# Batch 0's q and k loaded as float32 from SyncE's queue and cast on chip, in a dilated sliding-window attention with a SiLU feed-forward layer

## The chip, the cores and the metric

The kernel runs on one core of a Trainium2 chip. The metric is the device time of the kernel in microseconds (us), the median of three runs. Before the change it is 321.23 us (320.72 to 321.88). The profiled execution of the kernel before has a span of 319.5 us, and TensorE was granted its full clock in it. Line numbers (L127) are those of the kernel before.

## What is computed

Attention over 8 batches, 8 heads, 576 positions and 64 features, followed by a feed-forward layer over the 4608 tokens (model width 512, inner width 2048). All inputs and the output are float32.

```python
rel = pos[:, None] - pos[None, :]
mask_plain = (rel >= 0) & (rel < 32)                       # heads 0 to 3
mask_dil = (rel >= 0) & (rel < 128) & (rel % 4 == 0)       # heads 4 to 7
scores = where(mask, q @ k.T / sqrt(64), -1e9)
attn_out = softmax(scores) @ v
x = attn_out.transpose(0, 2, 1, 3).reshape(4608, 512)
h = x @ w_in
out = (h / (1 + exp(-h))) @ w_out
```

## The kernel before, in words

**Work and data.** Everything on chip is float16, and matmuls accumulate in float32. Attention goes batch by batch. The plain heads work in blocks of 96 queries against 128 keys. The dilated heads are split into the four residues of the position modulo 4, so that a dilated window of 128 becomes a plain window of 32 among 144 positions (`M`). The feed-forward layer goes over groups of 512 tokens, of which the first is split in two of 256 (`GROUPS`). For each group, layer 1 makes 16 blocks of `h` (L861, four matmuls each), ScalarE takes the tanh (L870), VectorE makes `gT` (L872), and layer 2 (L894) needs all 16 blocks of `gT` and `w_out`.

**Batch 0.** Its q and k are loaded by GpSimd's DMA queue with a cast from float32 to float16 on the way (`issue_part`, L125). `issue_first` (L131, called at L191 and L192) loads rows 0 to 95 (`MA`) of the 144 for the dilated heads and then for the plain heads, k before q; `k0` (L226) loads the last 48 rows of both into one tile, the "rest". TensorE transposes these tiles against the identity: `TD` (L529, `trans_d0`) for the dilated heads, `TA` (L554, `trans_a0`) for the plain ones, `TR` (L540) and `TS` (L567) for the rest. Batch 0's masks come as a bias that a matmul with the identity adds to the scores (L595). The scores are exponentiated by ScalarE (L616, L620), multiplied with V (L656) and divided (L659, L660), and the result is transposed into `xA` (L698, L710), the input of layer 1.

**Loads and their order.** GpSimd issues all loads of the first part of the run, in the order of the program: q and k of batch 0, the identity and the band of the masks (made by GpSimd itself), a first half of V for the dilated heads (`vraw`, L200), V for the plain heads (`vp`, L201), and then the list `ORDER` (L55, walked from L216): `k0` the rest of q and k, `r0` the second half of `vraw`, `w0a` to `w3` the four parts of `w_in`, `c0` a cast-free copy of the second half of `vraw` into the tile `vd` on GpSimd (L232), `d1` and `p1` q and k of batch 1 (dilated and plain heads), `r1` and `v1` its V, and `o0` to `o3` the parts of `w_out`. The instruction at L232 waits for the transfer of `r0`, and everything that stands behind it in GpSimd's program waits with it. Batch 2 is loaded by `third_batch` at the end of batch 0. Batches 3 to 7 take another path: their q and k are cast into DRAM (L137) and read back transposed by SyncE (L151, L154).

**The plan.** While the program is built, a planner fixes the order of the instructions: it keeps an estimated time, takes the next step that its estimates say is ready, and chooses ScalarE or VectorE for copies by which of them would be done first (`best`, L483). When loads land is part of these estimates: `LOAD_US` and `AT_W0` (L56, L57) give the landing times of the list, and `AT_DIL`, `AT_PLAIN`, `AT_VRAW`, `AT_VP`, `AT_REST`, `AT_V1` (L332 to L338) those of the first loads. On the chip every engine runs its instructions in the planned order and waits where an estimate was too early. Batch 0's own order of steps is the list at L721: `TD`, `S` (scores), `TA`, `V` (the copy into `vd`), `D` and `P` (the products with V of the dilated and plain heads), `XD` and `XP` (the transposes into `xA`), `TR`, `TS`.

Of the kernel before, what the change touches and what calls it, by code (L numbers as in the profile page):

```python
# [16 lines left out]
def kernel(  # L17
# [9 lines left out]
    nc = tc.nc  # L27
# [26 lines left out]
    BIG = 32768.0  # L54
    ORDER = "k0 r0 w0a w0b c0 w1 w2 w3 d1 p1 r1 o0 v1 o1 o2 o3".split()  # L55
    LOAD_US = {"w": 2.75, "o": 2.6, "d": 3.7, "p": 3.7, "r": 1.4, "v": 2.6, "k0": 2.0, "r0": 1.2, "c0": 0.0, "w0a": 1.4, "w0b": 1.4}  # L56
    AT_W0 = 10.6  # L57
    BIASED = (0,)
# [35 lines left out]
    kPs = [cpool.tile([P, HP // 2, W + S], F16, name=f"kP_{i}") for i in range(2)]  # L94
    pairs = {
        key: cpool.tile([MA, HP // 2, DIL, 2, D], F16, name=f"pair_{key}")
        for key in ("k", "q", "rest")
    }
    fence = cpool.tile([P, 4], F16, name="fence")
# [6 lines left out]
    def nat_of(b, key):  # L106
        i = ("k", "q", "rest").index(key)
        return nats[b % 2][:MA, i * RW : (i + 1) * RW].rearrange("p (h r d) -> p h r d", h=H, r=DIL)
# [15 lines left out]

    def issue_part(src, m0, m1, dst, h0, h1):  # L125
        rows = src[0].rearrange("h (m r) d -> m h (r d)", r=DIL)
        nc.gpsimd.dma_start(  # L127
            out=dst[: m1 - m0, h0:h1].rearrange("p h r d -> p h (r d)"), in_=rows[m0:m1, h0:h1]
        )

    def issue_first(h0, h1):  # L131
        issue_part(k, 0, MA, nat_of(0, "k"), h0, h1)
        issue_part(q, 0, MA, nat_of(0, "q"), h0, h1)

# [45 lines left out]

    for t in vraws[::-1]:
        nc.vector.memset(t, 0.0)
    nc.vector.memset(vps[0][:W, 0, :], 0.0)
    nc.vector.memset(kqDs[0][:, :, :, 0, MA:], 0.0)
    for t in vps:
        nc.vector.memset(t[:, :, D:], 1.0)
    for t in vds:
        nc.vector.memset(t[:, :, :, :, D:], 1.0)
    for t in kPs:
        nc.vector.memset(t[:, :, :W], 0.0)  # L190
    issue_first(HN, H)  # L191
    issue_first(0, HN)  # L192
    make_identity(nc, ident)
    nc.gpsimd.memset(band, 1.0)
    for s, base in ((1, 0), (-1, W - 1)):
        nc.gpsimd.affine_select(
            out=band, in_=band, compare_op=ALU.is_ge, fill=0.0, base=base,
            pattern=[[s, P]], channel_multiplier=-s,
        )
    issue_vraw(0, (0,))  # L200
    issue_vp_first()  # L201
    nc.vector.tensor_scalar(band, band, 1.0, BIG, ALU.subtract, ALU.mult)
    nc.vector.tensor_copy(mask_d[:, :6], band[:, None, :MH].broadcast_to([P, 6, MH]))
    nc.vector.tensor_copy(mask_d[:, 6:], band[:, None, P - MH :].broadcast_to([P, 4, MH]))
    nc.vector.tensor_copy(mask_p, band[:, None, W:].broadcast_to([P, 6, QB]))
    nc.vector.memset(mask_p[:W, :2], -BIG)
    for t in probs:
        c = 2 * 4 * MH
        n = PW + P - c
        nc.scalar.copy(t[:, c:], vraws[1].rearrange("p a h r d -> p (a h r d)")[:, :n])  # L210

    wi = moe_w_in.rearrange("(c p) f -> p c f", p=P)
# [3 lines left out]
    for what in ORDER:  # L216
        kind, n = what[0], int(what[1])
        if kind == "w":
            f0, f1 = {"": (0, 4), "a": (0, 2), "b": (2, 4)}[what[2:]]
            cols = slice((4 * n + f0) * P, (4 * n + f1) * P)  # L220
            nc.gpsimd.dma_start(out=w_in16[:, :, cols], in_=wi[:, :, cols])  # L221
        elif kind == "o":
            nc.gpsimd.dma_start(
                out=w_out16[:, 4 * n : 4 * n + 4], in_=wo[:, 4 * n : 4 * n + 4]
            )
        elif what == "k0":  # L226
            issue_part(k, MA, M, nat_of(0, "rest"), 0, H)
            issue_part(q, MA, M, nat_of(0, "rest")[MR:], 0, H)
        elif what == "r0":
            issue_vraw(0, (1,))  # L230
        elif what == "c0":
            nc.gpsimd.tensor_copy(vds[0][:, 1, :, :, :D], vraws[0][:, 1])  # L232
        elif kind == "d":
            issue_nat(n, HN, H)
        elif kind == "p":
            issue_nat(n, 0, HN)
        elif kind == "r":
            issue_vraw(n)
        else:
            issue_vp(n)  # L240
        at += LOAD_US[what] if what in LOAD_US else LOAD_US[kind]
        AT[what] = at
        if kind == "w":
            for f in range(f0, f1):
                AT_WIN[4 * n + f] = at
# [18 lines left out]
    class Plan:  # L264
        def __init__(self):
            self.t = 0.0
            self.now = 0.0
            self.free = {"ACT": 0.0, "DVE": 0.0}
            self.heap = []
            self.n = 0  # L270
            self.rings = {nm: [] for nm in RINGS}
# [59 lines left out]
    t2 = at  # L331
    AT_DIL = {0: 5.4, 1: AT["d1"], 2: t2 + 7.0}  # L332
    AT_PLAIN = {0: 7.5, 1: AT["p1"], 2: t2 + 7.0}
    AT_VRAW = {0: 8.6, 1: AT["r1"], 2: t2 + 8.6}
    AT_VP = {0: 10.6, 1: AT["v1"], 2: t2 + 11.4}
    AT_CAST = t2 + 18.0
    AT_REST = AT["k0"]
    AT_V1 = AT["r0"] + 1.2  # L338
    AT_WOUT = [AT[f"o{n}"] for n in range(4)]
# [96 lines left out]
    def attention(b):  # L436
# [91 lines left out]

        def trans_d0(ring, h):  # L529
            tps = small(ring, [P, 4, MA], F16, f"td_{b}_{h}")  # L530
            for n in range(4):
                nc.tensor.transpose(
                    tps[:, n],
                    nat_of(b, "kq"[n % 2])[:, HN + h, n // 2 * 2 : n // 2 * 2 + 2, :], ident[:MA, :MA],
                )
            step = best(0.34, 0.42)
            yield step
            copy_on(step[0], kqD[:, h].rearrange("p r k m -> p (r k) m")[:, :, :MA], tps)

# [101 lines left out]
        def vd_of(ab):  # L641
            if b == 0 and ab == 1:
                return
            step = best(0.335, 0.95) if pe_path else ("DVE", 0.335)
            yield step
            copy_on(step[0], vd[:, ab, :, :, :D], vraws[b % NV][:, ab])
# [73 lines left out]
        if b == 0:  # L720
            order = [  # L721
                ("TD", 0), ("TD", 1), ("TD", 2), ("TD", 3), ("S", 3), ("S", 4), ("TA", 0, "k"),
                ("TA", 1, "k"), ("TA", 0, "q"), ("TA", 1, "q"), ("V", 0), ("D", 0, 0), ("D", 0, 1),
# [30 lines left out]
        for key in order:  # L754
# [9 lines left out]
            elif kind == "TA" and b == 0:  # L764
                st = Step(
                    lambda ring, a=a: trans_a0(ring, *a), 0.36, rings,
                    [AT_PLAIN[0]],
                )
            elif kind == "TD" and b == 0:
                st = Step(lambda ring, a=a: trans_d0(ring, *a), 0.17, rings, [AT_DIL[b]])  # L770
            elif kind == "TR":
                st = Step(lambda ring: trans_d1(ring), 0.34, rings, [AT_REST])
            elif kind == "TS":
                st = Step(lambda ring, a=a: trans_a1(ring, *a), 0.36, rings, [AT_REST])
            elif kind == "TA":
# [227 lines left out]
```

## Time and profile before

| engine or queue | busy in the span of 319.5 us |
|---|---|
| TensorE (PE), matmuls | 299.9 us (94%) |
| VectorE (DVE) | 195.1 us (61%) |
| ScalarE (ACT) | 163.6 us (51%) |
| GpSimd (POOL) | 54.5 us (17%), 87 instructions |
| DMA | 44.49 MB moved, 139 GB/s on average |

| stretch, us | TensorE busy | VectorE busy | ScalarE busy | GpSimd busy |
|---|---|---|---|---|
| 0 to 5 | 0.00 | 2.42 | 4.18 | 3.67 |
| 5 to 10 | 2.12 | 1.17 | 2.34 | 4.93 |
| 10 to 15 | 5.00 | 1.83 | 3.07 | 1.71 |
| 15 to 20 | 4.13 | 2.82 | 3.96 | 1.75 |
| 20 to 25 | 3.96 | 4.02 | 3.58 | 4.84 |
| 25 to 30 | 4.26 | 3.73 | 3.63 | 1.02 |
| 30 to 35 | 3.00 | 2.75 | 1.89 | 3.41 |
| 35 to 40 | 4.19 | 4.88 | 4.22 | 5.00 |

The page and the trace show one execution. "Busy" is the time in which an engine had an instruction under way; DMA issues on GpSimd are shown as instructions of about 0.7 us each. Matmuls overlap, so a busy TensorE need not be at its peak. A casting load is counted by the bytes that it writes, which are half of those that it reads. The chain of waits is followed back from the last instruction to what released each step; the waits view lists for each line what ended its idle time. The first transposes of batch 0 (L532) start at 5.26 us, the first scores (L595) at 9.98, the first matmul of layer 1 (L861) at 20.30 and the first of layer 2 (L894) at 41.12.

### The profile page before, as it was taken

How to read it: one execution, taken by the hardware profiler on the slowest of the kernel's cores; microseconds unless marked ns; L12 is line 12 of the kernel's file. 1: busy time of each engine (PE TensorE's matmuls, PEld its weight loads, DVE VectorE, ACT ScalarE, POOL GpSimd, SP SyncE). 2: the span in 40 equal slices, each digit the busy share in tenths (PEclk: the TensorE clock that was granted, in tenths of full speed). 3: DMA queues.
4: the chain of work that ended last, by engine and by line, in shares of the span. 5: the costliest groups of instructions: out<-in, count | busy, mean ns of one | idle time of the engine just before them, and what ended most of it. 6: DMA issues, size and time to landing. Idle time of an engine off the chain costs nothing.

```text
span 319.5 us, 6092 instructions
## 1 busy us (share of the span) xinstructions
PE 299.9 (94%) x2378; PEld 152.7 (48%) x2378; DVE 195.1 (61%) x493; ACT 163.6 (51%) x300; POOL 54.5 (17%) x87
## 2 busy tenths in 40 slices
PE   2797689999999999999999999999999999999994
PEld 1466575655445444544454444444444444444442
DVE  4367798899679777843895787548841553355000
ACT  7586665566665365453563564546452453355111
POOL 8473923000900031004100500000000000000000
PEclk9999999999999999999999999999999999999999
DMA  7999999999999959997999799952191000100221
GB/s 90 157 130 202 197 191 199 209 202 169 100 203 208 224 108 190 208 201 143 184 236 209 130 193 173 212 129 73 51 182 42 28 35 33 66 33 2 81 83 66
DMA packets 107124, 44.49 MB, mean 139 GB/s; under 512 B 73304, under 2 KB 102488, under 8 KB 107096
## 3 DMA queue, kind: packets, MB, share of 16 engines
q0 software_dynamic: 48960, 19.92, 51.6%
q1 hardware_dynamic: 52952, 14.75, 26.3%
q10 hardware_dynamic: 5184, 9.44, 8.4%
q8 instruction: 18, 0.29, 0.4%
q14 instruction: 10, 0.08, 0.1%
HBM read 39.84 MB, written 18.28 MB: 182 GB/s over the span
## 4 chain that ended last, share of the span: by engine, by line
PE 84%; DMA 8%; POOL 4%; ACT 2%; DVE 1%; issue 1%; ACTq 0%; POOLq 0%
PE y L894 38%; PE h L861 36%; PE s L607 3%; DMA w_in<-in_moe_w_in_dram 3%; DMA vraw<-in_v_dram 3%; DMA w_out<-in_moe_w_out_dram 2%; PE av_p L656 2%; PE av_d L656 2%; POOL nat L127 1%; ACT ob L905 1%; POOL vraw L161 1%; POOL vp L179 0%; POOL w_in L221 0%; DVE gT L872 0%; PE td L518 0%
## 5 line engine op out<-in xcount | busy, mean ns | idle before, releaser
L894 PE MATMUL y<-w_out,gT 128*128 128x512 f16 x576 | 138.6, 379 | 1.7 <-ACT ob L905 1.1
L872 DVE SCALAR_TENSOR_TENSOR gT<-th,h 128x512 f16<-128x512 f32 (+1 forms) x160 | 98.6, 628 | 59.3 <-ACT th L870 59.1
L870 ACT ACTIVATE th<-h 128x512 f32<-128x512 f32 (+1 forms) x160 | 88.4, 555 | 82.0 <-PE h L861 78.0
L861 PEld LDWEIGHTS <-w_in 128*128 128x128 f16 x640 | 58.0, 97 | 56.9 <-DMA w_in<-in_moe_w_in_dram 3.0
L894 PEld LDWEIGHTS <-gT 128*128 128x128 f16 x576 | 53.8, 98 | 61.2 <-issue 2.0
L861 PE MATMUL h<-xR,w_in 128*128 128x512 f16 x320 | 78.0, 379 | 0.2 <-DVE gT L872 0.2
L861 PE MATMUL h<-xA,w_in 128*128 128x512 f16 (+1 forms) x320 | 65.4, 337 | 3.0 <-DMA w_in<-in_moe_w_in_dram 2.1
L616 ACT ACTIVATE probs<-s 128x768 f16<-128x768 f32 (+2 forms) x47 | 36.5, 776 | 19.4 <-PE s L607 16.8
L905 ACT ACTIVATE ob<-y 128x512 f32<-128x512 f32 x36 | 21.5, 598 | 39.9 <-PE y L894 39.8
L660 DVE TENSOR_TENSOR oD<-av_d,rcps 72x256 f16<-72x256 f32 x64 | 26.9, 420 | 2.2
L656 PEld LDWEIGHTS <-probs 128*128 128x128 f16 x448 | 22.1, 99 | 11.9 <-issue 0.4
L660 DVE TENSOR_TENSOR oP<-av_p,rcps 96x256 f16<-96x256 f32 x48 | 20.2, 420 | 1.6
L397 POOL COPY fence<-kqT 128x1 f16<-128x1 f16 x10 | 2.0, 206 | 97.5 <-DMA kqT<-kq_s 97.5
L659 DVE RECIPROCAL rcps<-av_p 96x4 f32<-96x4 f32 x48 | 8.3, 174 | 13.1 <-PE av_p L656 12.7
L625 DVE TENSOR_TENSOR probs<-probs,mask_p 128x768 f16<-128x768 f16 x21 | 11.6, 552 | 6.0 <-ACT probs L616 5.9
L656 PE MATMUL av_d<-vd,probs 128*128 128x65 f16 x256 | 14.2, 196 | 0.3 <-ACT qP L479 0.3
L659 DVE RECIPROCAL rcps<-av_d 72x4 f32<-72x4 f32 x64 | 10.9, 171 | 5.0 <-PE av_d L656 5.0
L656 PE MATMUL av_p<-vp,probs 128*128 128x65 f16 x192 | 13.1, 194 | 0.2 <-ACT probs L620 0.2
L625 DVE TENSOR_TENSOR probs<-probs,mask_d 128x576 f16<-128x576 f16 (+1 forms) x23 | 11.8, 513 | 2.0 <-ACT probs L616 1.8
L161 POOL DMA_DIRECT2D vraw<-in_v_dram x16 | 11.0, 688 | 6.6 <-DVE rcps L659 2.3
L174 POOL DMA_DIRECT2D vp<-in_v_dram x7 | 10.0, 1431 | 2.1 <-PE av_p L656 1.8
L481 DVE COPY vd<-vraw 128x1024 f16<-128x1024 f16 x14 | 6.2, 440 | 4.5 <-DMA vraw<-in_v_dram 4.5
(86 smaller groups left out, 139.5 us busy)
## 6 DMA issues: line engine op xcount, KB each, us to landing
out_dram<-ob ACTq DMA_DIRECT2D x36, 256.0 KB, 3.7
kq_s<-in_k_dram POOLq DMA_DIRECT2D x5, 576.0 KB, 11.5
kq_s<-in_q_dram POOLq DMA_DIRECT2D x5, 576.0 KB, 15.1
vp<-in_v_dram POOLq DMA_DIRECT2D x7, 384.0 KB, 8.7
w_out<-in_moe_w_out_dram POOLq DMA_DIRECT2D x4, 512.0 KB, 11.4
vraw<-in_v_dram POOLq DMA_DIRECT2D x8, 224.0 KB, 5.6
w_in<-in_moe_w_in_dram POOLq DMA_DIRECT2D x3, 512.0 KB, 8.1
x_s<-oP SPq DMA_DIRECT2D x10, 144.0 KB, 3.8
```

Source lines behind the costliest of these rows:

```text
L161: nc.gpsimd.dma_start(out=vraw[p0 : p0 + m1 - m0, ab].rearrange("p h r d -> p h (r d)"), in_=src[m0:m1],)
L174: nc.gpsimd.dma_start(out=vps[b % NV][:, :, :D], in_=v_win(b * H * S - W, HN * NB, QB * D))
L616: nc.scalar.activation(p2, both[:, :, :n], AF.Exp, scale=scale)
L625: nc.vector.tensor_tensor(p2, p2, mk, ALU.mult)
L656: nc.tensor.matmul(a[:, i, : D + 1], lhs(i), rhs(i), start=True, stop=True)
L659: nc.vector.reciprocal(rcp[:n], a[:n, :, D : D + 1])
L660: nc.vector.tensor_tensor(o, a[:n, :, :D], rcp[:n, :, None].broadcast_to([n, HN, D]), ALU.mult)
L861: nc.tensor.matmul(h[:, :w], w_in16[:, c, f * P : (f + 1) * P], x_g[:, c], start=(c == 0), stop=(c == HP - 1),)
L870: nc.scalar.activation(th[:, :w], h[:, :w], AF.Tanh, scale=0.5)
L872: nc.vector.scalar_tensor_tensor(gTs[g][:, f, :w], th[:, :w], 1.0, h[:, :w], ALU.add, ALU.mult)
L894: nc.tensor.matmul(y, gTs[g][:, f, tb * P : (tb + 1) * P], w_out16[:, f], start=(f == 0), stop=(f == NFF - 1),)
L905: nc.scalar.activation(ob, y, AF.Copy, scale=0.5)
```

## The change

Batch 0's q and k are no longer loaded by GpSimd with a cast. SyncE's queue, which has no other work at that time, loads them as float32 with eight DMAs into six pieces of scratch (`stages`). The scratch is laid over tiles that are not used so early: the three `xR` tiles, the two `kqT` tiles and the tiles `pair`, which become one tile for that. On-chip casts then make the float16 tiles: four of them (rows 0 to 95: k and q of the dilated heads, k and q of the plain heads) are steps `C` of the plan, on VectorE or ScalarE; the two of the rest are `c4` and `c5`, on GpSimd, in the list behind `w3`. `k0` and `c0` leave the list; the second half of `vraw` is copied into `vd` by a step of the plan, as the first half is. The making of the mask tiles on VectorE is cut in two parts (steps `K`) that stand between the casts, and `TD` transposes k and q in separate steps, so that k can go ahead of q. The estimates of the plan are set anew. The purpose is to have GpSimd's queue issue only V and the weights, and to start its issues earlier.

```diff
...
-    ORDER = "k0 r0 w0a w0b c0 w1 w2 w3 d1 p1 r1 o0 v1 o1 o2 o3".split()
-    LOAD_US = {"w": 2.75, "o": 2.6, "d": 3.7, "p": 3.7, "r": 1.4, "v": 2.6, "k0": 2.0, "r0": 1.2, "c0": 0.0, "w0a": 1.4, "w0b": 1.4}
-    AT_W0 = 10.6
+    ORDER = "r0 w0a w0b w1 w2 w3 c4 c5 d1 p1 r1 o0 v1 o1 o2 o3".split()
+    LOAD_US = {"w": 2.6, "o": 2.6, "d": 3.1, "p": 3.1, "r": 1.4, "v": 2.5, "r0": 1.2, "w0a": 1.3, "w0b": 1.3, "c4": 0.0, "c5": 0.0}
+    AT_W0 = 9.8
+    AT_STAGE = (3.7, 4.9, 6.2, 7.6, 13.0, 14.5)
...
-    pairs = {
-        key: cpool.tile([MA, HP // 2, DIL, 2, D], F16, name=f"pair_{key}")
-        for key in ("k", "q", "rest")
-    }
+    pair_all = cpool.tile([MA, 3, HP // 2, DIL, 2, D], F16, name="pair_all")
+    pairs = {key: pair_all[:, i] for i, key in enumerate(("k", "q", "rest"))}
+    homes = [
+        xRs[0].rearrange("p a b -> p (a b)"),
+        xRs[1].rearrange("p a b -> p (a b)"),
+        xRs[2].rearrange("p a b -> p (a b)"),
+        kqTs[0].rearrange("p a b c -> p (a b c)"),
+        kqTs[1].rearrange("p a b c -> p (a b c)"),
+        pair_all.rearrange("p a b c d e -> p (a b c d e)"),
+    ]
+    stages = [
+        t[:MA, : 2 * HN * DIL * D].bitcast(F32).rearrange("p (h c) -> p h c", h=HN) for t in homes
+    ]
...
-    def issue_part(src, m0, m1, dst, h0, h1):
-        rows = src[0].rearrange("h (m r) d -> m h (r d)", r=DIL)
-        nc.gpsimd.dma_start(
-            out=dst[: m1 - m0, h0:h1].rearrange("p h r d -> p h (r d)"), in_=rows[m0:m1, h0:h1]
-        )
-
-    def issue_first(h0, h1):
-        issue_part(k, 0, MA, nat_of(0, "k"), h0, h1)
-        issue_part(q, 0, MA, nat_of(0, "q"), h0, h1)
+    def issue_first():
+        for n, (src, h0, m0, m1, p0) in enumerate(
+            ((k, HN, 0, MA, 0), (q, HN, 0, MA, 0), (k, 0, 0, MA, 0), (q, 0, 0, MA, 0),
+             (k, HN, MA, M, 0), (q, HN, MA, M, MR), (k, 0, MA, M, 0), (q, 0, MA, M, MR))
+        ):
+            rows = src[0].rearrange("h (m r) d -> m h (r d)", r=DIL)
+            dst = stages[n if n < 4 else 2 + n // 2]
+            nc.sync.dma_start(out=dst[p0 : p0 + m1 - m0], in_=rows[m0:m1, h0 : h0 + HN])
...
-    for t in vraws[::-1]:
-        nc.vector.memset(t, 0.0)
-    nc.vector.memset(vps[0][:W, 0, :], 0.0)
-    nc.vector.memset(kqDs[0][:, :, :, 0, MA:], 0.0)
-    for t in vps:
-        nc.vector.memset(t[:, :, D:], 1.0)
-    for t in vds:
-        nc.vector.memset(t[:, :, :, :, D:], 1.0)
-    for t in kPs:
-        nc.vector.memset(t[:, :, :W], 0.0)
-    issue_first(HN, H)
-    issue_first(0, HN)
+    issue_first()
...
+    for t in vraws[::-1]:
+        nc.vector.memset(t, 0.0)
+    nc.vector.memset(vps[0][:W, 0, :], 0.0)
+    for t in vps:
+        nc.vector.memset(t[:, :, D:], 1.0)
+    for t in vds:
+        nc.vector.memset(t[:, :, :, :, D:], 1.0)
+    for t in kPs:
+        nc.vector.memset(t[:, :, :W], 0.0)
     issue_vraw(0, (0,))
     issue_vp_first()
-    nc.vector.tensor_scalar(band, band, 1.0, BIG, ALU.subtract, ALU.mult)
-    nc.vector.tensor_copy(mask_d[:, :6], band[:, None, :MH].broadcast_to([P, 6, MH]))
-    nc.vector.tensor_copy(mask_d[:, 6:], band[:, None, P - MH :].broadcast_to([P, 4, MH]))
-    nc.vector.tensor_copy(mask_p, band[:, None, W:].broadcast_to([P, 6, QB]))
-    nc.vector.memset(mask_p[:W, :2], -BIG)
...
+
+    def finish_consts(n):
+        if n:
+            nc.vector.tensor_copy(mask_p, band[:, None, W:].broadcast_to([P, 6, QB]))
+            nc.vector.memset(mask_p[:W, :2], -BIG)
+            nc.vector.tensor_copy(mask_d[:, 6:], band[:, None, P - MH :].broadcast_to([P, 4, MH]))
+        else:
+            nc.vector.memset(kqDs[0][:, :, :, 0, MA:], 0.0)
+            nc.vector.tensor_scalar(band, band, 1.0, BIG, ALU.subtract, ALU.mult)
+            nc.vector.tensor_copy(mask_d[:, :6], band[:, None, :MH].broadcast_to([P, 6, MH]))
+
+    def cast_stage(copy, n):
+        key = ("k", "q", "k", "q", "rest", "rest")[n]
+        h0 = (HN, HN, 0, 0, HN, 0)[n]
+        copy(
+            nat_of(0, key)[:, h0 : h0 + HN].rearrange("p h r d -> p h (r d)"), stages[n],
+        )
...
-        elif what == "k0":
-            issue_part(k, MA, M, nat_of(0, "rest"), 0, H)
-            issue_part(q, MA, M, nat_of(0, "rest")[MR:], 0, H)
+        elif kind == "c":
+            cast_stage(nc.gpsimd.tensor_copy, n)
         elif what == "r0":
             issue_vraw(0, (1,))
-        elif what == "c0":
-            nc.gpsimd.tensor_copy(vds[0][:, 1, :, :, :D], vraws[0][:, 1])
...
-            self.free = {"ACT": 0.0, "DVE": 0.0}
+            self.free = {"ACT": 5.7, "DVE": 3.7}
...
-    AT_DIL = {0: 5.4, 1: AT["d1"], 2: t2 + 7.0}
-    AT_PLAIN = {0: 7.5, 1: AT["p1"], 2: t2 + 7.0}
-    AT_VRAW = {0: 8.6, 1: AT["r1"], 2: t2 + 8.6}
-    AT_VP = {0: 10.6, 1: AT["v1"], 2: t2 + 11.4}
+    AT_DIL = {1: AT["d1"], 2: t2 + 7.0}
+    AT_PLAIN = {1: AT["p1"], 2: t2 + 7.0}
+    AT_VRAW = {0: 6.8, 1: AT["r1"], 2: t2 + 8.6}
+    AT_VP = {0: 9.0, 1: AT["v1"], 2: t2 + 11.4}
     AT_CAST = t2 + 18.0
-    AT_REST = AT["k0"]
-    AT_V1 = AT["r0"] + 1.2
+    AT_V1 = AT["r0"]
...
-        def trans_d0(ring, h):
-            tps = small(ring, [P, 4, MA], F16, f"td_{b}_{h}")
+        def staged(n):
+            step = best(0.62, 0.95)
+            yield step
+            cast_stage(nc.scalar.copy if step[0] == "ACT" else nc.vector.tensor_copy, n)
+
+        def consts_of(n):
+            yield "DVE", (0.85, 0.75)[n]
+            finish_consts(n)
+
+        def trans_d0(ring, g, nm):
+            tps = small(ring, [P, 4, MA], F16, f"td_{b}_{g}_{nm}")
             for n in range(4):
+                h = 2 * g + n // 2
                 nc.tensor.transpose(
-                    tps[:, n],
-                    nat_of(b, "kq"[n % 2])[:, HN + h, n // 2 * 2 : n // 2 * 2 + 2, :], ident[:MA, :MA],
+                    tps[:, n], nat_of(b, nm)[:, HN + h, n % 2 * 2 : n % 2 * 2 + 2, :],
+                    ident[:MA, :MA],
...
-            copy_on(step[0], kqD[:, h].rearrange("p r k m -> p (r k) m")[:, :, :MA], tps)
+            copy_on(
+                step[0],
+                kqD[:, 2 * g : 2 * g + 2, :, "kq".index(nm), :MA].rearrange("p h r m -> p (h r) m"),
+                tps,
+            )
...
-            if b == 0 and ab == 1:
-                return
...
-                ("TD", 0), ("TD", 1), ("TD", 2), ("TD", 3), ("S", 3), ("S", 4), ("TA", 0, "k"),
+                ("C", 0), ("K", 0), ("C", 1), ("TD", 0, "k"), ("TD", 1, "k"), ("TD", 0, "q"), ("TD", 1, "q"),
+                ("C", 2), ("S", 3), ("S", 4), ("C", 3), ("K", 1), ("TA", 0, "k"),
...
-                    [AT_PLAIN[0]],
-                )
+                    [steps["C", "kq".index(a[1]) + 2], steps["K", 1]],
+                )
+            elif kind == "C":
+                st = Step(lambda ring, a=a: staged(*a), 0.0, (), [AT_STAGE[a[0]]], ())
+            elif kind == "K":
+                st = Step(lambda ring, a=a: consts_of(*a), 0.0, (), [steps["C", a[0]]], ())
             elif kind == "TD" and b == 0:
-                st = Step(lambda ring, a=a: trans_d0(ring, *a), 0.17, rings, [AT_DIL[b]])
+                st = Step(
+                    lambda ring, a=a: trans_d0(ring, *a), 0.17, rings,
+                    [steps["C", "kq".index(a[1])]],
+                )
             elif kind == "TR":
-                st = Step(lambda ring: trans_d1(ring), 0.34, rings, [AT_REST])
+                st = Step(lambda ring: trans_d1(ring), 0.34, rings, [AT_STAGE[4]])
             elif kind == "TS":
-                st = Step(lambda ring, a=a: trans_a1(ring, *a), 0.36, rings, [AT_REST])
+                st = Step(lambda ring, a=a: trans_a1(ring, *a), 0.36, rings, [AT_STAGE[5]])
...
```

## The prediction

> **What bounds the kernel now.** I read the whole span first, then its start, then the stream of loads. In the answer by stretches of time (columns: stretch, its length, TensorE busy, clock, DMA share, GB/s) TensorE is full from 60 us on and loses time only before:
>
> ```profile
> 0.00:20.00 20.00, 11.26 (x170) 1.00 1.13 125
> 20.00:40.00 20.00, 15.40 (x197) 1.00 1.27 186
> 40.00:60.00 20.00, 18.61 (x237) 1.00 1.54 198
> 60.00:100.00 40.00, 40.00 (x395) 1.00 1.31 180
> ```
>
> That is 8.7 + 4.6 + 1.4 = 14.7 us idle of 19.6 in the whole run. Busy flatters a pipelined TensorE, so I also count work: four 512-column matmuls take 0.86 us in the chain, 0.42 ns a column. By columns the timeline's TensorE rows hold 7.2 us of work up to 20 us, 20.8 up to 40, 37.5 up to 60, and then about 0.93 us per us. Against 0.93, 12.3, 5.4 and 2.1 us are lost in the three stretches: 20 us is the room. Work after 60 us is the same in both kernels, so the end moves by what the start gains.
>
> What sets the start is in the chain that ended last, cut to 0 to 45 us (start, length, piece):
>
> ```profile
> 1.38 1.41 POOL nat L127 x2
> ...
> 8.24 1.23 POOL nat L127 x2
> 9.47 8.72 DMA vraw<-in_v_dram
> ...
> 18.25 1.04 POOL vd L232
> 19.29 1.41 POOL w_in L221 x2
> 20.70 9.73 DMA w_in<-in_moe_w_in_dram
> ...
> 33.50 7.58 DMA w_out<-in_moe_w_out_dram
> ...
> 41.12 1.02 PE y L894 x4
> ```
>
> But for 1.5 us of layer 1 at 30.5, up to 41 us it is loads, issues on GpSimd, and one GpSimd cast (L232, `c0`) in the middle of the issues. The waits of 0 to 60 us say what that cast does (total, times, longest):
>
> ```profile
> POOL vd L232 <- DMA vraw<-in_v_dram: 6.5, 1, 6.5
> PE h L861 <- DMA w_in<-in_moe_w_in_dram: 2.1, 3, 1.0
> PE ta_k L558 <- DMA nat<-in_k_dram: 1.9, 1, 1.9
> PE td L518 <- DMA nat<-in_q_dram: 1.6, 1, 1.6
> ```
>
> GpSimd sits 6.5 us on a V load with the last three w_in issues and all of batch 1's behind it. The DMA view of 0 to 24 us, 40 slices of 0.6 us, shows the stream running dry:
>
> ```profile
> GB/s 0 0 0 0 7 49 150 193 198 132 125 148 158 141 167 114 107 145 152 155 154 166 176 175 168 189 193 195 197 216 118 52 18 13 32 31 191 208 198 208
> ```
>
> From 18.0 to 21.6 us the six slices sum to 264, where 24 to 56 us has a mean of 197. So 3.6 - 0.6 x 264/197 = 2.8 us of transfer time are lost. From 3.0 to 18.0 us the mean is 158; at 197 those bytes would take 12.1 us instead of 15, another 2.9 us at most.
>
> **What the Trainium skill says.** "DMA: Bandwidth & Descriptors", section "SWDGE vs HWDGE vs iDMA": a DMA that casts must be issued from GpSimd, so loads on SyncE's queue arrive as float32 and need casts. Same page, "Issuing engines are not separate DMA queues": all issuers share the same 16 DMA engines, and a second issuer saves only issue time. I therefore book no bandwidth for the second queue, only the holes. The trace of before has no SyncE load at the start to compare. "SBUF — State Buffer", section "SBUF: two separate sides": a VectorE fp32 copy in its two-port mode locks GpSimd out, and GpSimd's descriptors wait. In before each issue costs about 0.67 us even beside VectorE memsets, so no such stall shows. Four copies of 0.7 us would hold it 2.8 us at most, which the slack ahead of w3 (below) covers.
>
> **The change, part by part.**
>
> *Six GpSimd issues and the `c0` cast go.* Four issues at about 0.67 us (L127, 1.38 to 4.16) = 2.8 us ahead of the identity; two more at 0.65 = 1.3 us; then the 6.5 us wait and 1.04 us. The V and weight issues left take 0.65 + 0.55 + 1.50 + 0.74 + 1.53 + 2.23 = 7.2 us behind 1.5 us of identity and band. Started near 1.0, w3 is issued by about 9.7 instead of 21.4. The V half that `c0` cast falls to VectorE (0.42 to 0.49 in before's L481 rows) or ScalarE (1.04, its L479 row): hidden, since neither is over 65% busy from 8 to 20 us.
>
> *Eight float32 loads on SyncE.* 2.36 MB of float32, as many bytes as the casting loads read. Does a plain float32 write cost more than a cast? Queues in the page's section 3:
>
> ```profile
> q0 software_dynamic: 48960, 19.92, 51.6%
> q10 hardware_dynamic: 5184, 9.44, 8.4%
> ```
>
> q0 counts fp16 bytes, so per float32 MB it takes 51.6 / 39.8 = 1.3% of the engines; q10, the plain float32 stores, takes 0.9%. The rows here are 1 KB and not 2 KB, so I take equal cost: 0. The bad bound is that the 1.18 MB more written count in full at 197 GB/s: 6.0 us. The first load can be issued at about 0.8 instead of 1.38: 0.5 us gained. Each of the first four is 0.39 MB, 1.0 us at 2 x 197 and 1.25 at 2 x 158. Before's first load needed 3.9 us from issue to use. So they land at about 4.2, 5.3, 6.5 and 7.6.
>
> *Casts of 96x1024.* Four on VectorE or ScalarE. VectorE from float32 is not in the trace. The price in "VectorE: DVE Perf Modes", "The perf-mode tier table" (2x, about 150 cycles fixed) gives an estimate of (150 + 512)/0.96 = 0.69 us; 1.2 if the mode is missed. ScalarE about 1.04. Only the first two lie on the path to the transposes: first transpose at 4.2 + 0.7 + a hop = 5.0 (5.26 before), the last of TD near 7 (7.6). The moved band and mask operations (0.20 + 0.41 + 0.22 before the q cast) push it by under 1 us. The scores gain more: before, they stand behind TA, which waits 1.9 us, and start at 9.98; now near 7.5. V and vp are issued 2.4 to 3 us earlier. I expect the first layer-1 matmul at 16.5 to 18 instead of 20.3.
>
> *GpSimd casts `c4`, `c5`, each 1.04 by L232's row.* Behind them wait d1 and all later issues, and TensorE's TR and TS. The rest of k and q should land at 11 to 14 us on the shared engines; both casts end by 16. By then 2 MB of w_in are in flight, over 8 us of stream, so waiting d1 opens no hole.
>
> *Sum.* The loads that the chain follows to 41 us gain 2.8 (hole) + half of the 2.9 (1.5) + 0.5 (first issue) = 4.8 us. Half, because vp's 128-byte rows stay slow. On TensorE the start gains 2.3 to 3.8 us and the w_in waits shrink, so it can follow. 321.2 - 4.8 = 316.4. With none of the 2.9 and no early issue it is 318.4; with all of it 315.0.
>
> **The rivals.**
>
> *TensorE's own start holds it.* Casts, hops and the dependent steps of batch 0 may bring layer 1 forward by only 1 us, and batch 1 may then come too soon to be used. For: before, TensorE works in short pieces from 10 to 20 us. Against: the chain has no batch 0 compute until 30 us. Gain 1.5: 319.7.
>
> *Slower.* The float32 writes cost their size: -6.0 + 4.8 = -1.2, 322.4. Or `c4` waits as long as `c0` did and TensorE's fixed order stands at TR for those 6.5 us: -6.5 + 4.8 = -1.7, 322.9. For: no load of this kind is in the trace, and one cast already blocked GpSimd once. Against: q10's share, and SyncE's queue has nothing ahead of these loads. I take 322.7.
>
> *More than the loads.* Early w_in, V and w_out also close TensorE's idle 1.4 us between 40 and 60 us, and the stream runs at 197 throughout: 4.8 + 1.4 + 1.4 = 7.6, 313.6. Against: those gaps are mostly hand-overs between engines.
>
> **How the numbers follow.** Forecast around 316.4: 0.53; TensorE-bound, 319.7: 0.17, of which 0.05 falls within 0.3%; more: 0.14; slower: 0.13; no change at all: 0.03. Faster by over 0.3% (under 320.3): 0.53 + 0.12 + 0.14 = 0.79; within: 0.05 + 0.03 = 0.08; slower: 0.13. The range runs from 313.2, inside the best case, to 320.9, which takes in the TensorE-bound case and leaves the slower one and the far end of the best out.
>
> **What would show it.** Right: no GpSimd wait on a V load, w3 issued near 10 us, no slices under 100 GB/s between 5 and 40 us, first layer-1 matmul before 18, first w_out matmul at 36 to 37 instead of 41.1, and TensorE full from about 55. Wrong: float32 packets that hold the stream under 158 GB/s counted as fp16, `c4` ending after 20 us, or TensorE waiting at TR or at a cast for over 1 us. If w_out comes 4 us earlier and the end does not, the step from loads to end is the one that failed.

## The result, and the profile after

The changed kernel takes 323.76 us (323.25 to 324.25), the kernel before beside it 320.98 (320.70 to 321.88): a ratio of 1.0082, 95% interval 1.0055 to 1.0108. It is slower by 0.8%, where 1.5% faster (4.8 of 321.2 us) was forecast. The profiled span grows from 319.5 to 322.6 us. Lines of the changed kernel are numbered anew: layer 1 is L896, layer 2 L929, batch 1's transposes `TD` L533, the on-chip casts L227.

By stretches of time (stretch, length, TensorE busy with the number of matmuls, granted clock, DMA share, GB/s) the changed kernel:

```profile
0.00:20.00 20.00, 9.18 (x121) 1.00 1.30 187
20.00:40.00 20.00, 16.52 (x229) 0.91 1.44 197
40.00:60.00 20.00, 19.90 (x242) 1.00 1.53 198
60.00:100.00 40.00, 39.94 (x394) 1.00 1.27 181
```

The first stretch has 2.1 us less of busy TensorE; the second has more, but at a granted clock of 0.91 in place of 1.00. (The trace has no record of the clock before 19.49 us, and the view shows that as 1.00; a matmul of 384 columns took 302 ns then, 0.79 ns a column, and those of 256 columns 108 ns at 36.7 us, 0.42.) So I count work again, by columns at 0.42 ns, every matmul of the trace with at least 64 columns:

| work done by, us | 20 | 25 | 30 | 35 | 60 | 180 | 190 | 300 |
|---|---|---|---|---|---|---|---|---|
| before | 7.2 | 10.7 | 14.3 | 17.0 | 37.6 | 152.7 | 162.3 | 269.8 |
| changed | 5.2 | 8.9 | 12.2 | 14.2 | 36.4 | 152.1 | 159.8 | 266.6 |

The change is 2 us of work behind at 20 us, 2.8 at 35, 1.2 at 60 and 0.6 at 180. It loses 1.9 more between 180 and 190, where layer 1 waits for `xR`, and is 3.2 behind at 300. The waits of TensorE after 60 us have that one (total, times, longest):

```profile
PE h L896 <- DMA xR<-x_s: 1.8, 1, 1.8
```

The stream of loads is what was forecast in one respect. In the DMA view of 0 to 24 us (slices of 0.6 us) the hole is gone:

```profile
GB/s 0 0 0 114 188 374 254 258 234 251 265 248 244 234 196 152 150 207 249 200 161 189 185 156 155 156 183 192 195 198 194 197 202 230 196 203 201 207 207 207
```

No slice after the start falls under 150. But the first slices, about 250, are float32 bytes; as float16 they are 125, less than the 158 of before. And the chain that ended last, up to 45 us, has changed its shape:

```profile
7.29 3.23 POOL w_in L240 x4
10.51 3.93 issue
...
14.46 0.71 POOL w_in L240
...
15.52 2.03 POOL nat L227 x2
17.55 1.87 POOL nat L130 x3
...
19.44 12.38 DMA nat<-in_q_dram
...
31.95 0.63 PE td L533 x11
```

Before, this stretch was a V load and then w_in, with layer 1 behind it. Now it is batch 1's q, and TensorE's next step is not layer 1 but batch 1's `TD`. Four of the waits of 0 to 60 us show the rest (total, times, longest):

```profile
DVE vd L496 <- DMA vraw<-in_v_dram: 5.1, 1, 5.1
POOL w_in L240 <- DMA vraw<-in_v_dram: 3.9, 1, 3.9
PE ta_q L587 <- DVE nat L227: 3.1, 1, 3.1
PE td L533 <- DMA nat<-in_q_dram: 2.1, 1, 2.1
```

V is late: it was to come earlier. Its landing also holds `w3`, the last part of w_in, which has no use for V. The trace shows why: GpSimd's loads take eight semaphores in turn, and a load is issued only when the one eight places before it has landed. `w3` is the ninth load, and the first half of V is the first, landed at 14.17 us; `c4`, `c5` and batch 1's loads stand behind `w3`. V's copy runs at 14.19 us (11.47 before), and the cast of the plain heads' q stands behind that copy on VectorE, as the timeline of both engines shows (start, length, instruction, and in brackets the idle time ahead of it):

```profile
14.19 0.43 DVE L496 COPY vd<-vraw 128x1024 f16<-128x1024 f16 x1 [5.11 <-DMA vraw<-in_v_dram]
14.53 0.68 DVE L227 CAST nat<-kqT 96x1024 f16<-96x1024 f32 x1
15.27 0.85 PE L587 MATMUL ta_q<-ident,nat 96*64 96x96 f16 x16 [3.11 <-DVE nat L227]
```

So there were three suspects: V's load behind SyncE's queue, or behind VectorE's casts; the order that the plan gives to VectorE and TensorE; and TensorE's clock.

### The profile page after: what moved, and what is told of

The parts are those of the page before. It is cut to its first block, busy times and chain, and to the rows that moved or that the text cites. A ratio compares the mean times of both kernels' runs of the same rounds, so it can differ in the third digit from the quotient of the medians.

```text
span 322.6 us, 6109 instructions
## 1 busy us (share of the span) xinstructions
PE 301.7 (94%) x2378; PEld 154.0 (48%) x2378; DVE 196.2 (61%) x494; ACT 165.3 (51%) x304; POOL 52.8 (16%) x82
## 4 chain that ended last, share of the span: by engine, by line
PE 79%; DMA 6%; DVE 4%; POOL 4%; issue 2%; ACT 2%; SPq 1%; ACTq 0%; DVEq 0%; POOLq 0%
PE h L896 36%; PE y L929 35%; DMA nat<-in_q_dram 4%; PE s L636 3%; PE av_d L683 2%; DMA xR<-x_s 2%; PE av_p L683 2%; DVE gT L907 1%; POOL w_in L240 1%; SPq L163 1%; DVE oD L687 1%; PE td L533 1%; ACT ob L940 1%; POOL nat L227 1%; ACT probs L645 1%
## 5 line engine op out<-in xcount | busy, mean ns | idle before, releaser
L929 PE MATMUL y<-w_out,gT 128*128 128x512 f16 x576 | 138.1, 379 | 0.0
L896 PEld LDWEIGHTS <-w_in 128*128 128x128 f16 x640 | 58.7, 98 | 56.1 <-issue 2.4
L929 PEld LDWEIGHTS <-gT 128*128 128x128 f16 x576 | 54.1, 98 | 59.8
L896 PE MATMUL h<-xR,w_in 128*128 128x512 f16 x320 | 77.9, 379 | 2.4 <-DMA xR<-x_s 1.8
L896 PE MATMUL h<-xA,w_in 128*128 128x512 f16 (+1 forms) x320 | 66.9, 341 | 0.1
L686 DVE RECIPROCAL rcps<-av_p 96x4 f32<-96x4 f32 x48 | 8.4, 174 | 12.3 <-PE av_p L683 12.0
L683 PE MATMUL av_p<-vp,probs 128*128 128x65 f16 x192 | 12.4, 194 | 0.0
## 6 DMA issues: line engine op xcount, KB each, us to landing
kq_s<-in_k_dram POOLq DMA_DIRECT2D x5, 576.0 KB, 10.7
w_out<-in_moe_w_out_dram POOLq DMA_DIRECT2D x4, 512.0 KB, 11.4
```

Source lines behind the costliest of these rows:

```text
L683: nc.tensor.matmul(a[:, i, : D + 1], lhs(i), rhs(i), start=True, stop=True)
L686: nc.vector.reciprocal(rcp[:n], a[:n, :, D : D + 1])
L896: nc.tensor.matmul(h[:, :w], w_in16[:, c, f * P : (f + 1) * P], x_g[:, c], start=(c == 0), stop=(c == HP - 1),)
L929: nc.tensor.matmul(y, gTs[g][:, f, tb * P : (tb + 1) * P], w_out16[:, f], start=(f == 0), stop=(f == NFF - 1),)
```

## The experiments

Each was timed beside the kernel before; the ratio is to that kernel, with its 95% interval.

| run | what | us | ratio |
|---|---|---|---|
| e1 | before, without `c0` | 319.93 | 0.9981 (0.9963 to 0.9998) |
| e2 | before, plus SyncE's eight loads, unread | 327.01 | 1.0196 (1.0155 to 1.0236) |
| e3 | change, casts C on ScalarE | 324.00 | 1.0103 (1.0075 to 1.0130) |
| e4 | change, V's estimate 14.2 | 326.92 | 1.0193 (1.0165 to 1.0221) |
| e5 | change, four loads on SyncE | 323.21 | 1.0083 (1.0046 to 1.0120) |
| e6 | change, two loads on SyncE | 324.52 | 1.0107 (1.0079 to 1.0135) |
| e7 | change, TensorE kept busy in two waits | 323.27 | 1.0073 (1.0048 to 1.0097) |
| e8 | change, t2 later | 324.39 | 1.0112 (1.0072 to 1.0152) |
| e9 | change, AT_W0 13.8 | 318.79 | 0.9950 (0.9928 to 0.9972) |
| e10 | before, AT_W0 7.1 | 324.81 | 1.0123 (1.0096 to 1.0149) |
| e11 | e5, AT_W0 14.8 | 316.76 | 0.9870 (0.9844 to 0.9896) |
| e12 | e1, AT_W0 12.6 | 318.20 | 0.9928 (0.9910 to 0.9947) |
| e13 | before, AT_W0 12.6 | 319.25 | 0.9960 (0.9943 to 0.9977) |
| e14 | change, AT_W0 14.8 | 318.74 | 0.9963 (0.9943 to 0.9984) |

### One part alone: the copy off GpSimd's list (e1)

```diff
-    ORDER = "k0 r0 w0a w0b c0 w1 w2 w3 d1 ...
+    ORDER = "k0 r0 w0a w0b w1 w2 w3 d1 ...
...
-            nc.gpsimd.tensor_copy(vds[0][:, 1, :, :, :D], vraws[0][:, 1])
...
-            if b == 0 and ab == 1:
-                return
```

> The kernel before, with one part of the change alone: the GpSimd copy c0 is gone from the list of loads, and the plan copies that half of V on VectorE or ScalarE. q and k still come from GpSimd with a cast. If the hole in the stream of loads (2.8 us between 18.0 and 21.6 us in the kernel before) is worth its length, the w_in and w_out loads land about 2.8 us earlier (last quarter of w_in used first at 27.6 instead of 30.5, first w_out matmul at 38.3 instead of 41.1) and the time falls to about 318.4. If the early loads are not what sets the end, w_out comes earlier and the time stays within 1 us of 321.

Measured 319.93 us, 0.2% below the kernel before. The data of w_in had all moved at 28.1 us (30.0 before), those of the first part of w_out at 38.9 (40.7): 1.8 to 1.9 us of the expected 2.8, and a third of that in the time. The hole is real, but it is not worth its length at the end.

### Whose fault is V's late landing (e2, e3)

e2 puts the eight SyncE loads into the kernel before, with nothing that reads them and no cast. e3 takes the casts off VectorE.

```diff
 e2, with the scratch of the change
...
+    for n, (src, h0, m0, m1, p0) in enumerate(...):
...
+        nc.sync.dma_start(out=dst[p0 : p0 + m1 - m0], in_=rows[m0:m1, h0 : h0 + HN])
     issue_first(HN, H)
 e3
-            step = best(0.62, 0.95)
+            step = ("ACT", 0.95)
             yield step
             cast_stage(...)
```

> The kernel before, with the eight float32 loads of the change issued on SyncE as well, into the same scratch, where nothing reads them. No cast is added on VectorE. Queue theory (loads that SyncE has queued hold the DMA engines and GpSimd's queue gets little until they are nearly through): GpSimd's first load, which is used at 5.3 us in the kernel before, lands at 8 us or later, everything behind it moves by 5 to 8 us, time about 327 to 329. Lock theory (VectorE's copies keep GpSimd from writing its descriptors): VectorE is nearly idle here from 3.7 to 5.6 us, so both queues share from the start, GpSimd's first packets are at 2.9 us as before, the first load lands near 6.5 and the time is about 323 to 325.

> The changed kernel with all four casts C on ScalarE, so that VectorE is left with the masks only between 4.8 and 9 us. Lock theory: GpSimd's queue moves its first data near 6 to 7 us instead of 9.5, and the first half of V lands 2 to 3 us earlier than 14.2. Queue theory: first data still at 9.5 (within 0.5) and V still at 14; the time stays within 2 us of 323.8, as the casts take 1.04 instead of 0.69 us but no longer stand behind V's copy.

In e3 VectorE is idle from 4.24 to 7.26 us and GpSimd's queue still moves its first data at 9.40 us (9.51 in the changed kernel). The lock theory falls as a reason for this start. In e2 they start at 4.55 instead of 2.90, at a time when VectorE had done nothing but memsets, and after that both queues share. Neither theory had that: a queue that must wait for SyncE to finish would start at 15. It fits a third one: what SyncE had queued when GpSimd's first load was issued goes first, and what it queues later is shared with. In e2 GpSimd's first load is issued by 2.15 us, when SyncE has issued little over two loads; in the changed kernel by 4.17, when it has issued more than six. SyncE's queue had moved 621 rows of 1 KB by GpSimd's first data in e2 and 1753 in the changed kernel, of 2304 in all. e3's time, within 0.3 us of the changed kernel's (the intervals overlap), fits too.

### How much is queued ahead (e5, e6)

This backlog can be counted, so two versions with fewer SyncE loads test it. The loads taken off SyncE are casting loads of GpSimd again.

```diff
 e5
...
             ((k, HN, 0, MA, 0), (q, HN, 0, MA, 0), (k, 0, 0, MA, 0), (q, 0, 0, MA, 0),
-             (k, HN, MA, M, 0), (q, HN, MA, M, MR), (k, 0, MA, M, 0), (q, 0, MA, M, MR))
 e6, further
-             (k, 0, 0, MA, 0), (q, 0, 0, MA, 0))
...
     issue_vraw(0, (0,))
+    issue_part(k, 0, MA, nat_of(0, "k"), 0, HN)
+    issue_part(q, 0, MA, nat_of(0, "q"), 0, HN)
```

> The changed kernel with the last four of SyncE's eight loads (the rest of q and k) given back to GpSimd as two casting loads between vp and r0; c4 and c5 go with them, the plan's estimates stay. Backlog theory: what SyncE has queued when GpSimd's first load is issued goes first. At 4.2 us SyncE then has 4 x 24 = 96 rows per DMA engine issued and about 35 moved (242 rows a us over 16 engines since 1.9), so 61 rows or 4.1 us are ahead: first data of GpSimd's queue at about 8.2 instead of 9.5, and first V half used near 10 to 11 instead of 14.2. If GpSimd's queue starts at a time of its own, or waits for an empty SyncE queue in the same way as before, the first data stay at 9.5. First layer-1 matmul near 21 by the backlog theory; time 321 to 323.

> The changed kernel with only the dilated heads' k and q on SyncE; the plain heads' k and q and the rest are casting loads of GpSimd again (behind the first V half, and between vp and r0). Steps C2, C3, c4 and c5 are gone. Backlog theory: 48 rows per engine issued by SyncE, about 35 moved at 4.2 us, 13 rows or 0.9 us ahead: first GpSimd data at about 5.0, V used near 7.5, first layer-1 matmul near 17 to 18. If the start is what the change lost, the time falls to 319 to 320, at or below the kernel before; if loads bound it from 25 to 40 us anyway, it stays at 320 to 321.

The first data of GpSimd's queue moved at 7.82 and 4.88 us: expected were 8.2 and 5.0. V was copied at 10.50 and 8.99 us (14.19 in the changed kernel; 7.5 had been expected of e6). e5 is the test: its first data came 3.7 us after GpSimd's first issue had ended, when 1431 of SyncE's 1536 rows had moved. e6 decides little, since its 0.7 us are also what the kernel before took with no load on SyncE (2.17 to 2.90). The DMA view of 2 to 9 us shows it by queue (packets, MB, share). The changed kernel has SyncE's queue alone:

```profile
q1 hardware_dynamic: 1721, 1.69, 104.0%
```

and with two loads on SyncE GpSimd's has the larger part:

```profile
q0 software_dynamic: 1383, 0.59, 69.8%
q1 hardware_dynamic: 779, 0.77, 41.0%
```

The first line also prices the float32 loads: 1721 rows in 7 us, 246 a us. The same 1 KB of float32, cast on the way, moves at up to 380 rows a us later in the same trace, and at 309 by the 158 GB/s of the first stretch before. At 246, all 2304 rows take 9.4 us; at 380 they would take 6.1 and at 309 7.5. Whether the float32 write or the other queue makes the difference was not tested.

The times did not follow, 323.21 and 324.52. Layer 1 began at 21.1 us in e6 (17 to 18 expected) and at 19.7 in e5, ahead of the kernel before, and at 25 us e5 had done 12.1 us of work, 1.4 more than it. At 30 us it had done 12.2. So had the changed kernel, e6, e8 and, without its extra transposes, e7: all of them stop at 12.2. The timeline of e5 shows at what (L902 is layer 1, L539 batch 1's `TD`):

```profile
23.89 1.03 PE L902 MATMUL h<-xA,w_in 128*128 128x256 f16 x8
...
28.56 0.22 PE L539 MATMUL td<-ident,nat 96*128 96x96 f16 x1 [2.98 <-DMA nat<-in_k_dram]
30.30 1.04 PE L539 MATMUL td<-ident,nat 96*128 96x96 f16 x11 [1.53 <-DMA nat<-in_q_dram]
31.14 1.05 PE L902 MATMUL h<-xA,w_in 128*128 128x256 f16 x4
```

TensorE stands for batch 1's k and q, with layer 1 behind it in its fixed order and w_in there. The start and V are not what the change lost.

### Three other edits (e4, e7, e8)

```diff
 e4
-    AT_VRAW = {0: 6.8, ...
+    AT_VRAW = {0: 14.2, ...
 e7, in trans_a0 and, with 36, in trans_d of batch 1
+            if nm == "q" and hp == 0:
+                for n in range(32):
+                    nc.tensor.transpose(tps[:, n % DIL], ident[:MA, :], ident[:MA, :MA])
 e8
-    t2 = at
+    t2 = at + 4.75
```

> The changed kernel with one estimate set to what its profile shows: the first half of V lands at 14.2 us instead of 6.8. The plan then puts V's copy on VectorE behind the cast of the plain heads' q, which in the changed kernel runs only at 14.5 because the copy in front of it waits for V. If this order costs time, TA of q moves from 15.3 to about 11, the plain heads' scores no longer wait for it, the first layer-1 matmul moves from 23.4 to about 21.5, and the time falls by 1 to 2 us to about 322. If V itself sets the start, layer 1 stays within 0.7 us of 23.4 and the time within 1 us.

> The changed kernel with 32 extra transposes of the identity on TensorE ahead of TA of the plain heads' q (where it waits from 12.2 to 15.3 us), and 36 ahead of the first TD of batch 1 (where it waits from 29.9 to 32.0). They write what the real transposes overwrite, and change nothing in the result. Clock theory: the waits cost more than their length, because TensorE's granted clock comes late (19.5 instead of 14.6 us) and falls to a half from 33.1 to 36.6 after the second wait. Then full clock comes by 16 to 17 us, the fall is gone, and the time drops by 1 to 2 us. If the clock does not matter for the end: within 0.5 us of the changed kernel, or longer by the extra transposes (68 x 0.1 us where they do not fit into the waits).

> The changed kernel with one number of the plan moved: t2, from which the plan takes the landing times of batch 2 and of the first cast into DRAM, is later by 4.75 us, as it was in the kernel before. SyncE's queue then has batch 3's first store ahead of batch 4's transposes again, as before. If the 1.8 us wait of TensorE for xR at 185.8 us comes from that order, it is gone and the time falls by 1.5 to 2.5 us to about 321.5 to 322. If it comes from the start's delay, it stays and the time with it.

e4 was to gain 1 to 2 us and lost 3, although V came 1.4 us earlier (copied at 12.82): its layer 1 began at 24.5, and its plan puts batch 1's first `TD` behind only 16 layer-1 matmuls, where the changed kernel has 28, e3 24 and the kernel before 60. That row of numbers gave the next experiment. e7 is inconclusive: full clock came at 17.96 instead of 19.49 us, but the half clock after the second wait stayed (31.6 to 35.0), and its interval overlaps the changed kernel's. In e8's profile the wait for `xR` near 185 us is gone, yet its five runs scatter from 322.39 to 326.16 and the interval takes in the changed kernel's ratio. SyncE's order alone does not make that wait: e7 issues SyncE's DMAs in the changed kernel's order, and its profile has no such wait either. What makes it stays open.

### The estimates of the plan (e9, e10)

One number each. `AT_W0` is where the plan starts counting the landing times of the list of loads. The times of batch 2's loads and of the first cast into DRAM are counted from the end of that list and move with it; e8 moved these alone, without a gain.

```diff
 e9, the changed kernel
-    AT_W0 = 9.8
+    AT_W0 = 13.8
 e10, the kernel before
-    AT_W0 = 10.6
+    AT_W0 = 7.1
```

> The changed kernel with one number changed: AT_W0 is 13.8 instead of 9.8, so that the plan takes all loads from r0 on to land 4 us later. In the changed kernel TensorE's fixed order has batch 1's first transposes (TD) behind 28 layer-1 matmuls, and it stands there for k and q of batch 1 until 31.95 us; in the kernel before they are behind 60. With 13.8 they are behind 60 again. Plan theory (the loss comes from the estimates, which are about 7 to 8 us early at d1 in the changed kernel and 5 in the one before): the 25 to 35 us stretch does 4 to 5 us of work again, and the time falls by 2.5 to 4 us, to 320 to 321.3. Start theory (V's late landing and the late layer 1 make the loss): layer 1 still starts at 23.4 and the time stays above 322.5.

> The kernel before with one number changed: AT_W0 is 7.1 instead of 10.6, so that the plan takes the loads from the list to land 3.5 us earlier than it did. No load, copy or queue changes. Batch 1's first TD then stands behind 28 layer-1 matmuls, as in the changed kernel, and the first layer-2 matmul behind 56 instead of 92. Plan theory: TensorE waits for batch 1's k and q from about 28 to 33 us with layer 1 queued behind, loses 2.5 to 4 us of work, and the time is 323 to 324.5, like the changed kernel's. Start theory: within 1 us of 320.8, as nothing about the start or the loads is different.

Both ways, the estimates decide. e9 falls to 318.79 us, more than expected, with the same loads, V still late (landed at 13.29 us) and layer 1 from 22.9 us. e10 rises to 324.81, 4.4 us above the kernel before and no faster than the changed kernel, with nothing of the change in it. The timeline of e10 around the place:

```profile
25.48 0.44 PE L698 MATMUL xp<-ident,oP 96*128 96x96 f16 x4
30.89 0.26 PE L518 MATMUL td<-ident,nat 96*128 96x96 f16 x1 [4.97 <-DMA nat<-in_k_dram]
32.95 1.04 PE L518 MATMUL td<-ident,nat 96*128 96x96 f16 x11 [1.80 <-DMA nat<-in_q_dram]
33.78 1.05 PE L861 MATMUL h<-xA,w_in 128*128 128x256 f16 x4
```

and that of e9, where 32 layer-1 matmuls stand in the same stretch:

```profile
28.62 3.66 PE L896 MATMUL h<-xA,w_in 128*128 128x256 f16 x32
32.11 0.68 PE L533 MATMUL td<-ident,nat 96*128 96x96 f16 x12
```

The loads that e10 waits for were not late: they landed at 30.84 to 32.81 us, 0.6 to 0.9 us earlier than in the kernel before. The plan was early. The changed kernel's plan has d1 at 9.8 + 1.2 + 2 x 1.3 + 3 x 2.6 + 3.1 = 24.5 us, and TensorE got batch 1's q at 31.95, 7.4 later. The kernel before has it at 28.55 and got it at 33.59, 5.0 later; with 60 layer-1 matmuls ahead of `TD`, it stood for less time:

```profile
30.48 1.49 PE L861 MATMUL h<-xA,w_in 128*128 128x256 f16 x12 [0.41 <-DMA w_in<-in_moe_w_in_dram]
31.80 0.21 PE L518 MATMUL td<-ident,nat 96*128 96x96 f16 x1
33.59 0.63 PE L518 MATMUL td<-ident,nat 96*128 96x96 f16 x11 [1.58 <-DMA nat<-in_q_dram]
```

The loads came 1.6 us earlier; the plan was told 4.05.

The wait also goes with a fall of the clock. In all eight runs that have the first `TD` behind 28 layer-1 matmuls or fewer (the changed kernel, e3 to e8, e10), the granted clock was a half for 3.4 to 6.8 us in or after the wait; in the other eight it did not fall once it was full. In the changed kernel it was a half for 3.41 us, which by an estimate, half of that time, is at most 1.7 us of work. Standing and clock were not priced apart.

e9 also has no wait for `xR`. Of its lead over the changed kernel, 2.7 us of work are there by 180 us (154.8 against 152.1) and 3.1 come later. The first part is the wait for batch 1, with the clock that fell after it; for the second only the new order as a whole is shown. Against the kernel before, the larger part of the changed kernel's deficit in its trace, 2.6 of 3.2 us, is of the second kind.

### With the order put right, what are the parts worth (e11 to e14)

```diff
 e11: e5 with         AT_W0 = 14.8     (first TD of batch 1 behind 72 layer-1 matmuls)
 e12: e1 with         AT_W0 = 12.6     (80)
 e13: before with     AT_W0 = 12.6     (80)
 e14: change with     AT_W0 = 14.8     (72)
```

> The version with four loads on SyncE (e5) and AT_W0 at 14.8: batch 1's first TD stands behind 72 layer-1 matmuls. In e5 layer 1 began at 19.7 us, 0.6 ahead of the kernel before, the last of w_in's data moved at 26.7 instead of 30.0 and w_out's first at 37.4 instead of 40.7, and TensorE had done 12.1 us of work by 25 us instead of 10.7, before it stood for batch 1. Plan theory: with that wait filled by layer 1 it stays ahead by 1.4 us or more; time 317.5 to 319.5, below both kernels. Start theory: no better than e5, 322 to 323.5.

> The kernel before without c0 (e1) and AT_W0 at 12.6 instead of 10.6: batch 1's first TD behind 80 layer-1 matmuls instead of 60. Plan theory: e1's TensorE had 3.95, 3.46 and 3.39 us busy of each 5 from 25 to 40 us, part of it the wait for batch 1's q; with layer 1 ahead of it 0.5 to 1.5 us are won, time 318.5 to 319.5. If e1's remaining gaps there are waits for w_in, none is won: 319.9.

> The kernel before with AT_W0 at 12.6 instead of 10.6, and nothing else: batch 1's first TD behind 80 layer-1 matmuls, as in e12. If later estimates alone are worth what e12 gained, the time is about 318.5; if the order only pays once the hole in the loads is gone, as TensorE in the kernel before waits for w_in from 24 to 31 us, it stays at 320 to 321. So e12's gain of 2.2 us is split between the estimate and c0.

> The changed kernel with AT_W0 at 14.8, the value of e11, and the same places in the order (first TD of batch 1 behind 72 layer-1 matmuls, first layer-2 matmul behind 108), but all eight loads on SyncE. If e11's further 2 us come from its queue (layer 1 from 18.9 instead of 22.9, w_out's data 1.6 us earlier), this stays at 318 to 319; if they come from the estimate, it falls to 317.

A later estimate alone gains 1.3 us in the kernel before (e13, 319.25). Without `c0` it is 318.20 (e12), so `c0` is worth about 1 us more (the two intervals just meet). The whole change with late estimates is 318.74 to 318.79 (e9, e14), no clear step from e13: the intervals overlap. With only four loads on SyncE it is 316.76 (e11), 1.3% below the kernel before and the best of all. e11 and e14 have the same places in the order, so those 2 us come with the four loads, and the two GpSimd casts that go with them, not with the estimate. (e14's executions spread from 317.81 to 322.47 us; the profiled one was among the longest, with full clock only from 27.6 us.) e11 by stretches:

```profile
0.00:20.00 20.00, 12.12 (x196) 1.00 1.35 190
20.00:40.00 20.00, 17.50 (x217) 1.00 1.48 191
```

and what its chain holds of loads up to 48 us:

```profile
4.68 8.09 DMA vp<-in_v_dram
...
13.05 14.09 DMA w_in<-in_moe_w_in_dram
...
27.43 5.46 DMA nat<-in_q_dram
...
33.70 14.37 DMA w_out<-in_moe_w_out_dram
```

By its chain the loads bound this kernel from 4.7 to 48 us, as the forecast took it for the changed one; in the changed kernel the order did (e9).

## Why the prediction was wrong

**"The first layer-1 matmul at 16.5 to 18", "V and vp are issued 2.4 to 3 us earlier".** Wrong. They were issued 2.0 to 2.2 us earlier and V was copied 2.7 later, because SyncE's backlog went first (e2, e5). I had taken from "DMA: Bandwidth & Descriptors", section "Issuing engines are not separate DMA queues", that all share the 16 engines, and read it as sharing evenly. The page says that they interleave; here GpSimd's first load was not served for 5.3 us after its issue, and the measurement decides. Layer 1 began at 23.39.

**"I take equal cost: 0" for the float32 loads.** Wrong, by the test that the forecast had named: the stream fell under 158 GB/s counted as float16, to about 125. At the measured rate 2304 rows take 9.4 us and not 6.1 to 7.5, 1.9 to 3.3 more. The row that I priced it by, the 2 KB stores of the output, was no stand-in for 1 KB rows. Of the 4.8 us this leaves 1.5 to 2.9; the first w_out matmul ran at 39.56 instead of 41.12, 1.6 earlier. So this term of the sum was mis-sized. The part on the hole of 2.8 us was right: it is gone.

**"w3 is issued by about 9.7", "no GpSimd wait on a V load".** Wrong: 14.45, after 3.9 us of waiting for V's landing. The working let GpSimd's issues follow one another, and had no line for the ninth load's wait for the first. **`c4`, `c5` "end by 16".** 17.55, with no new hole in the stream, as forecast. **The cast on VectorE, 0.69 us.** Right: 0.69, by the price of "VectorE: DVE Perf Modes", "The perf-mode tier table"; ScalarE 1.04, GpSimd 1.04 to 1.06.

**"On TensorE the start gains 2.3 to 3.8 us and the w_in waits shrink, so it can follow."** This is the step that failed, the one from loads to end. The working has a line for every load, cast and copy, and none for the plan's new estimates, which the diff sets anew and which fix the order of TensorE. They put batch 1's first `TD` behind 28 layer-1 matmuls instead of 60. Estimates that put it there make a slowdown of 4.4 us with nothing else changed (e10), and later ones turn the change into a gain (e9). The rival "slower" had the right kind of cause, TensorE's fixed order standing at a step whose data are late, but at `TR` and behind `c4`, which is not where it stood. That its 322.7 us lie near the measured 323.76 is therefore luck. Its other half, the float32 writes, cost a third to a half of its bound of 6.0 us.

**"Work after 60 us is the same in both kernels, so the end moves by what the start gains."** The work is the same, the end does not follow: the deficit was 1.2 us at 60 us and 3.2 at 300. The estimates also fix the order after the start. What in that order makes the later loss stays open.

**Slips in the working.** Against 0.93 us of work per us, the three stretches fall short by 11.4, 5.0 and 1.9 us, not by 12.3, 5.4 and 2.1; the table above has 0.97 per us from 60 to 300 us. And 0.8 + 3.9 us put the first load at 4.7, not 4.2: its cast ran at 4.78, the first transposes at 5.53 and the first scores at 8.66 (7.5 forecast, 9.98 before). Neither slip made the miss.

**The range** ended at 320.9, and the cost of a misplaced step, 4 to 5 us by e9 and e10, was in none of the cases that it took in.

## What to carry to other kernels

Where a planner's estimates fix the order of an engine, changed estimates are an edit of their own: compare where each engine stands in its order for which load, and move the estimates by as much as the loads really move. Queue few loads on a second DMA queue ahead of what the first queue needs soon: count the rows that stand in front. Price a load per row of its size and type from the nearest load, not from a store.

## What the runs showed of the hardware

- **A queue's backlog goes first.** GpSimd's first data moved 0.7, 0.7, 3.7 and 5.3 us after the end of its first issue, with none, two, four and eight loads on SyncE (at 2.90, 4.88, 7.82 and 9.51 us; the issue ended at 2.17 in the first case and at 4.17 in the others).
- **Eight of GpSimd's loads under way.** In these programs the ninth is issued when the first has landed: `w3` at 14.45 us, V's first half having landed at 14.17.
- **Float32 rows of 1 KB.** 246 a us on SyncE's queue without a cast, up to 380 a us on GpSimd's with a cast to float16 on the way.
- **TensorE's clock.** In the changed kernel the granted clock became full at 19.5 us (14.6 before), and it fell to a half for 3.4 us from 33.1, after the wait that ended at 31.95. In e10 it was a half for 6.8 us from 30.7, late in a wait of 4.97 us that one of 1.80 us followed. "TensorE: Matmul & The Clock Gate", section "Part 1: The HAM clock gate", has activity windows of about 3.4 us, and the lengths of 3.41 and 6.83 us agree. It puts the fall after a whole idle window; here waits of 0.36 and 2.05 us, with one matmul between them, were enough. The kernel before had a wait of 1.58 us at the same place and no fall.
- **VectorE and GpSimd's issues hold each other.** The band operation took 0.95 us instead of 0.20, and ended with GpSimd's issue of `vp`. That issue, beside a cast on VectorE when it began, took 1.86 us; the third line is the same issue in e3, with the casts on ScalarE:

```profile
4.69 1.86 POOL L188 DMA_DIRECT2D vp<-in_v_dram  x1
5.59 0.95 DVE L221 TENSOR_SCALAR band<-band 128x128 f16<-128x128 f16 x1
...
4.68 1.49 POOL L188 DMA_DIRECT2D vp<-in_v_dram  x1
```

"SBUF — State Buffer", section "SBUF: two separate sides", tells of such a lock between the two. Here it fits delays of VectorE by 0.75 us and of GpSimd's issue by 0.4 us, and not the 5 us that GpSimd's first data were late (e3).
